# A fused lightning attention and SwiGLU block: dummy matmuls of 512 columns ahead of the first transposes split into four of 128, and three more tiny ones

## The chip, the cores and the metric

The kernel runs on one core of one Trainium2 chip. The metric is the device time of one execution in microseconds; the median of several runs is compared. A profiled execution has a span (from its first to its last instruction) and a time of its own, which is somewhat longer than the span.

## The reference

Attention with a decay per head runs over blocks of 64 positions; a state per head is carried from block to block. Its output goes through a SwiGLU feed-forward block. There are 4 batches, 8 heads, 768 positions and a head dimension of 64; the feed-forward block has 512 inputs, 1536 hidden units and 512 outputs. All inputs and the output are float32.

```
for b in range(12):                      # blocks of 64 positions
    intra = (qb @ kb.T) * Dmask          # Dmask[i,j] = lam**(i-j) for i >= j, else 0
    out_b = intra @ vb + (qb * lam**(pos+1)) @ kv_state
    kv_state = lam**64 * kv_state + (kb * lam**(63-pos)).T @ vb
x = out, as (3072, 512)
g = x @ w_gate
y = (g * sigmoid(g) * (x @ w_val)) @ w_out
```

## The kernel before

The kernel works in blocks of 128 positions and twelve groups, each a pair of blocks of one batch. A group's q and k are loaded in float32 (`load_fp32`, L115), cast to bf16 (`cast_half`, L296, for the first groups), transposed, multiplied into scores (`scores`, L350), masked on VectorE (L357), and multiplied with v (`intra`, L515). The sum over earlier blocks comes from a state per head (`upd_mm` at L408, `inter` at L502). The feed-forward block of earlier groups (gate at L558, value at L574, output at L593, L703 and L793) fills TensorE between the attention of later groups.

Each engine executes its instructions in the order in which the program lists them; the order is written out by hand. The instructions of the start are issued in this order:

- The loads of lam, q, k and v for groups 0 and 1, on the queues of SyncE and ScalarE.
- On TensorE: 30 tiny dummy matmuls (L181) that multiply a constant, 64 rows by 64 columns of weights with 8 moving columns, alternately on the two halves of the array; then `warm_up(2)`; then the matmul that spreads lam over the partitions (L183, the wait for the transfer of lam stands before it); then `warm_up(4)`.
- ScalarE takes the logarithm of lam (L195, L197) and makes the decay tables of q (`qdec`, L203); VectorE makes `dec` (L199) and casts the first half of q of group 0 (L296), and ScalarE casts the half of k.
- `pe_transpose(0, 0, warm=1)`: four transposes on TensorE of q (L312), one dummy matmul of 256 columns (L187), four transposes of k (L312). VectorE moves the q transposes to SBUF with the decay factor (L318), ScalarE moves those of k (L314).
- `scores(0, (0,), 3)`: three dummy matmuls of 256 columns (L187) and sixteen score matmuls (L350).

`warm_up` writes dummy results into a bank of PSUM that nobody reads. Each matmul in the program is two instructions on TensorE, a weight load (in the profile PEld) and the matmul itself (PE).

```
    warm = nc.const_aps.tensor(1.0, [128, 512], BF16)
    def warm_up(n, cols=512):
        b = bank()
        for _ in range(n):
            nc.tensor.matmul(b[:, 0:cols], warm[:, 0:128], warm[:, 0:cols], start=True, stop=True)
```

The functions that the change touches, with the line numbers of the profile:

Of the kernel before, what the change touches and what calls it, by code (L numbers as in the profile page):

```python
# [19 lines left out]
@with_exitstack  # L20
def kernel(
    ctx: ExitStack,
    tc: tile.TileContext,
    q: bass.AP,
    k: bass.AP,
    v: bass.AP,
    lam: bass.AP,
    moe_w_gate: bass.AP,
    moe_w_val: bass.AP,
    moe_w_out: bass.AP,  # L30
    out: bass.AP,
):
    nc = tc.nc
    with tc.manual_schedule():
        _body(ctx, tc, nc, q, k, v, lam, moe_w_gate, moe_w_val, moe_w_out, out)


def _body(ctx, tc, nc, q, k, v, lam, moe_w_gate, moe_w_val, moe_w_out, out):
# [46 lines left out]
    def bank():  # L85
        if fixed:
            primed[fixed[0]] = 0
            last_bank.insert(0, fixed[0])
            return banks[fixed.pop(0)]
        last_bank.insert(0, ring[0] % 8)  # L90
        b = banks[ring[0] % 8]
        primed[ring[0] % 8] = 0
        ring[0] += 1
        return b
# [48 lines left out]
# [4 lines that stand above are left out]
# [29 lines left out]

    lam_ps = bank()
    b = bank()
    for n in range(30):
        r = slice(n % 2 * 64, n % 2 * 64 + 64)  # L180
        nc.tensor.matmul(b[r, 0:8], warm[r, 0:64], warm[r, 0:8], start=True, stop=True, skip_group_check=True)  # L181
    warm_up(2)
    nc.tensor.matmul(lam_ps[:, 0:H], ones[:, 0:128], lam_row, start=True, stop=True)  # L183
    warm_up(4)
    def warm_into(b, n, cols=256):
        for _ in range(n):
            nc.tensor.matmul(b[:, 0:cols], warm[:, 0:128], warm[:, 0:cols], start=True, stop=True)  # L187
# [1069 lines left out]
```

## Time and profile before

| what | value |
|---|---|
| runs | 217.79, 217.82, 219.28 us; median 217.82 |
| profiled execution | 218.1 us, span 216.3 us |
| TensorE matmuls (PE) | busy 209.8 us, 97% of the span, 2813 instructions |
| TensorE weight loads (PEld) | busy 153.3 us, 2816 instructions |
| VectorE (DVE) | busy 149.5 us, 69% |
| ScalarE (ACT) | busy 129.1 us, 60% |
| GpSimd (POOL) | busy 92.3 us, 43% |
| dummies of L146 | 6 matmuls of 512 columns, 607 to 634 ns each |

Times in the profile are counted from the first instruction. A row of the timeline has the start, the length from the first start to the last end of a merged group, the engine, the line, the operation, the tiles (output before the arrow) and the number of instructions. Matmuls overlap: the length of a single one is longer than the distance from its start to that of the next, so how fast TensorE works is read from distances of starts. A clock row gives the clock that TensorE was granted, as far as it is recorded.

### The profile page before, as it was taken

To read this page: it belongs to the slowest core of one execution; us is meant where nothing else is said; L and a number is where in the kernel's file an instruction comes from. 1 tells how busy PE (TensorE), PEld (TensorE's weight loads), DVE (VectorE), ACT (ScalarE), POOL (GpSimd) and SP (SyncE) were. 2 spreads that over 40 slices of the span, in tenths; PEclk is the share of its full clock that TensorE was granted. 3 is DMA by queue.
4 is the path that set the end of the run, shared out by engine and by line. 5 is a ranking of instruction groups with operands and counts; after the bars stand their busy time and mean duration, and the time that the engine had idled before them with its cause. 6 is when DMAs were issued, how large, how long until landed. Compare 5 with 4: busy or idle time off the path is not lost.

```text
span 216.3 us, 6883 instructions
## 1 busy us (share of the span) xinstructions
PE 209.8 (97%) x2813; PEld 153.3 (71%) x2816; DVE 149.5 (69%) x267; ACT 129.1 (60%) x280; POOL 92.3 (43%) x126
## 2 busy tenths in 40 slices
PE   8899999999999999999999999999999999999994
PEld 4666455888887447666754545888888888888883
DVE  1774447576677989775478988886797379961760
ACT  5788577666545254638368478754872766636522
POOL 6684755818498240685962336510740022200200
PEclk9999999999999999999999999999999999999999
DMA  6999999999999878999678899481000500005014
GB/s 189 346 354 345 378 337 321 290 249 232 315 352 151 191 214 190 257 186 238 168 169 236 203 230 215 103 225 68 2 5 3 194 0 3 0 3 194 0 52 146
DMA packets 88320, 39.76 MB, mean 184 GB/s; under 512 B 57698, under 2 KB 83938, under 8 KB 88290
## 3 DMA queue, kind: packets, MB, share of 16 engines
q1 hardware_dynamic: 84978, 38.22, 64.9%
q10 hardware_dynamic: 3312, 1.11, 2.0%
q8 instruction: 22, 0.36, 0.7%
q14 instruction: 8, 0.07, 0.1%
HBM read 28.31 MB, written 6.29 MB: 160 GB/s over the span
## 4 chain that ended last, share of the span: by engine, by line
PE 73%; DVE 7%; DMA 6%; SPq 5%; ACT 3%; issue 2%; POOL 2%; POOLq 1%; DVEq 0%
PE bank L793 20%; PE bank L703 15%; PE bank L558 13%; PE bank L574 13%; DMA woraw<-in_moe_w_out_dram 4%; PE bank L593 4%; SPq L122 2%; DMA qraw<-in_q_dram 2%; SPq L247 2%; DVE ws L666 2%; DVE h L577 1%; PE bank L515 1%; PE bank L146 1%; DVE wt L623 1%; PE bank L502 1%
## 5 line engine op out<-in xcount | busy, mean ns | idle before, releaser
L577 DVE TENSOR_TENSOR h<-sil,bank 128x256 bf16<-128x256 bf16 (+1 forms) x67 | 34.8, 531 | 26.3 <-PE bank L574 18.0
L558 PE MATMUL bank<-xt,wg_sb 128*128 128x256 bf16 (+1 forms) x268 | 52.5, 319 | 0.0
L574 PE MATMUL bank<-xt,wv_sb 128*128 128x256 bf16 (+1 forms) x268 | 52.4, 319 | 0.0
L562 ACT ACTIVATE sil<-bank 128x256 bf16<-128x256 f32 (+1 forms) x67 | 31.7, 479 | 23.7 <-PE bank L558 16.8
L574 PEld LDWEIGHTS <-wv_sb 128*128 128x128 bf16 x268 | 26.0, 98 | 15.8 <-DVE wv_sb L988 0.5
L558 PEld LDWEIGHTS <-wg_sb 128*128 128x128 bf16 x268 | 25.2, 98 | 13.8 <-DVE xt L527 0.2
L258 POOL TENSOR_TENSOR v_s<-v,dec 128x512 bf16<-128x512 f32 (+1 forms) x18 | 24.1, 1356 | 24.0 <-DMA v<-in_v_dram 16.0
L733 POOL TENSOR_TENSOR h<-sil,es 128x512 bf16<-128x512 bf16 x6 | 7.0, 1163 | 50.0 <-ACT sil L730 50.0
L793 PEld LDWEIGHTS <-h 128*128 128x128 bf16 x240 | 23.3, 98 | 3.4 <-issue 0.3
L793 PE MATMUL bank<-wo_sb,h 128*128 128x256 bf16 x180 | 21.6, 273 | 0.1
L793 PEld LDWEIGHTS <-hs 128*128 128x128 bf16 x180 | 17.6, 98 | 2.9
L357 DVE TENSOR_TENSOR ssb<-bank,causal 128x512 bf16<-128x512 f32 x24 | 15.4, 681 | 1.8 <-PE bank L350 1.8
L745 DVE TENSOR_TENSOR bank<-bank,es 128x512 f32<-128x512 f32 x12 | 7.8, 693 | 11.4 <-PE bank L703 10.1
L703 PEld LDWEIGHTS <-ws 128*128 128x128 bf16 x144 | 13.8, 97 | 2.3 <-issue 0.2
L793 PE MATMUL bank<-wt,hs 128*128 128x256 bf16 x120 | 15.0, 272 | 0.0
L730 ACT ACTIVATE sil<-bank 128x512 bf16<-128x512 f32 x18 | 10.7, 596 | 7.0 <-POOL h L733 4.6
L463 POOL TENSOR_TENSOR kvf<-kvs,ups 128x256 f32<-128x256 f32 x8 | 6.5, 813 | 19.1 <-ACT ups L430 19.1
L733 DVE TENSOR_TENSOR h<-sil,bank 128x512 bf16<-128x512 bf16 x18 | 12.2, 682 | 1.4 <-ACT sil L730 1.4
L703 PE MATMUL bank<-xs,ws 128*128 128x256 bf16 x96 | 12.8, 272 | 0.0
L527 ACT CAST xt<-bank 128x512 bf16<-128x512 f32 x19 | 11.6, 658 | 2.0 <-PE bank L515 1.5
L463 POOL TENSOR_TENSOR kvf<-kvf,ups 128x256 f32<-128x256 f32 x16 | 12.2, 763 | 0.9
L703 PE MATMUL bank<-xt,wg_sb 128*128 128x256 bf16 x72 | 10.8, 273 | 0.2 <-ACT ups L430 0.2
(119 smaller groups left out, 361.3 us busy)
## 6 DMA issues: line engine op xcount, KB each, us to landing
out_dram<-osb SPq DMA_DIRECT2D x22, 256.0 KB, 2.1
v<-in_v_dram SPq DMA_DIRECT2D x18, 256.0 KB, 4.5
woraw<-in_moe_w_out_dram SPq DMA_DIRECT2D x6, 512.0 KB, 7.6
qraw<-in_q_dram SPq DMA_DIRECT2D x24, 128.0 KB, 3.2
wraw<-in_moe_w_gate_dram SPq DMA_DIRECT2D x5, 512.0 KB, 7.2
wraw<-in_moe_w_val_dram SPq DMA_DIRECT2D x5, 512.0 KB, 6.9
kraw<-in_k_dram SPq DMA_DIRECT2D x20, 128.0 KB, 3.1
kraw<-in_k_dram SPq DMA_DIRECT2D x4, 512.0 KB, 6.6
```

The lines of the kernel that those rows point to most:

```text
L258: eng.tensor_tensor(out=st[("vs", g)][:, h0:h1], in0=st[("v", g)][:, h0:h1].rearrange("p h (s d) -> p h s d", s=2), in1=vfac(g, h0, h1), o ...
L357: nc.vector.tensor_tensor(out=ssb[:, h2, 2 * c:2 * c + 2].rearrange("p a s n -> p a (s n)"), in0=sp[(c, h2)].rearrange("p (a x) -> p a x", ...
L463: nc.gpsimd.tensor_tensor(out=o, in0=f, in1=u, op=ALU.add)
L527: fns[r](out=xt[:, g % 2, :, r].rearrange("p h (m s) -> p h s m", s=2) if g < NAT0 else xt[:, g % 2, :, :, r * M:r * M + M], in_=op[r].rea ...
L558: nc.tensor.matmul(gp[:, 0:N], wg_sb[:, mc, fs], xt[:, b0 // 2:b1 // 2, mc].rearrange("p g b n -> p g (b n)"), start=(mc == 0), stop=(mc = ...
L562: nc.scalar.activation(sil[:, 0:N], gp[:, 0:N], AF.Silu)
L574: nc.tensor.matmul(vp[:, 0:N], wv_sb[:, mc, fs], xt[:, b0 // 2:b1 // 2, mc].rearrange("p g b n -> p g (b n)"), start=(mc == 0), stop=(mc = ...
L577: nc.vector.tensor_tensor(out=h_sb[:, fc % FH, b0:b1].rearrange("p b n -> p (b n)"), in0=sil[:, 0:N], in1=vp[:, 0:N], op=ALU.mult)
L703: nc.tensor.matmul(o[:, fi * 256:fi * 256 + 256], lhs(i, c, 2 * j + fi), rhs(c), start=(start and fi == 0 and c == 0), stop=(c == KH - 1), ...
L730: nc.scalar.activation(sil[key], src, AF.Silu)
L733: eng.tensor_tensor(out=h_of(half, r), in0=v3(sil[half, r]), in1=v3(src), op=ALU.mult)
L793: nc.tensor.matmul(o, lhs(f), rhs(f), start=(start and f == 0), stop=(f == FH - 1), skip_group_check=True)
```

## The change

Three tiny dummy matmuls are added to the 30, and each of the six dummies of 512 columns becomes four of 128. The number of dummy columns in `warm_up` stays (1,024 ahead of the lam matmul, 2,048 behind it); there are 18 more matmuls and 18 more weight loads of this kind, and three more of each of the tiny kind, 42 instructions in all.

```
     lam_ps = bank()
     b = bank()
-    for n in range(30):
+    for n in range(33):
         r = slice(n % 2 * 64, n % 2 * 64 + 64)
         nc.tensor.matmul(b[r, 0:8], warm[r, 0:64], warm[r, 0:8], start=True, stop=True, skip_group_check=True)
-    warm_up(2)
+    warm_up(8, 128)
     nc.tensor.matmul(lam_ps[:, 0:H], ones[:, 0:128], lam_row, start=True, stop=True)
-    warm_up(4)
+    warm_up(16, 128)
```

## The prediction, made before the change was run

> **What bounds the kernel now.** I read first the busy line of the page, because it says which engine could be bought anything.
>
> ```profile
> span 216.3 us, 6883 instructions
> PE 209.8 (97%) x2813; PEld 153.3 (71%) x2816; DVE 149.5 (69%) x267; ACT 129.1 (60%) x280; POOL 92.3 (43%) x126
> PEclk9999999999999999999999999999999999999999
> ```
>
> PE is busy in 97% of the span, so time can only come from what PE does, or from the 6.5 us in which it is idle. The clock row shows full speed everywhere, but it can't show the start: the durations of equal matmuls have to be read for that. The edit lies in the first 5 us, so next comes the timeline of PE there (start, length, line, operation).
>
> ```profile
> 0.84 0.96 PE L181 MATMUL bank<-const-bfloat16-1.0 64*64 64x8 bf16 x30 [0.84 <-PEq L1241]
> 1.74 1.03 PE L146 MATMUL bank<-const-bfloat16-1.0 128*128 128x512 bf16 x2
> 2.71 0.59 PE L183 MATMUL bank<-lam_row,ones 1*128 1x8 f32 x2
> 3.23 1.89 PE L146 MATMUL bank<-const-bfloat16-1.0 128*128 128x512 bf16 x4
> 4.91 0.63 PE L312 MATMUL bank<-ident,qk 128*128 128x128 bf16 x4
> 5.34 0.42 PE L187 MATMUL bank<-const-bfloat16-1.0 128*128 128x256 bf16 x1
> 5.55 0.63 PE L312 MATMUL bank<-ident,qk 128*128 128x128 bf16 x4
> 5.98 0.58 PE L187 MATMUL bank<-const-bfloat16-1.0 128*128 128x256 bf16 x3
> 6.86 0.42 PE L350 MATMUL bank<-qkt 64*64 64x128 bf16 x16 [0.30 <-ACT qkt L314]
> 7.21 0.62 PE L312 MATMUL bank<-ident,qk 128*128 128x128 bf16 x8
> 7.67 0.50 PE L187 MATMUL bank<-const-bfloat16-1.0 128*128 128x256 bf16 x3
> ```
>
> Two things are to be seen. PE has no gap of its own from 0.84 to 6.5, so whatever is put ahead of L312 moves L312. And PE runs at two speeds: four transposes (L312) take 0.43 us from 4.91 to the next row at 5.34, that is 107 ns each, while eight of them at 7.21 take 0.46 us to 7.67, 57 ns each. The 256-column dummies say the same: one takes 0.21 us from 5.34 to 5.55, three take some 0.33 at 7.67. The switch falls among the three dummies at 5.98. So the six 512-column dummies of L146 run at the slow rate, about 0.42 us each (1.68 us from 3.23 to 4.91 for four).
>
> The third view is the chain of waits that ends last, cut to the first 8 us (start, length, what).
>
> ```profile
> 0.84 0.96 PE bank L181 x30
> 1.81 0.97 PE bank L146 x2
> 2.78 0.52 PE bank L183 x2
> 3.30 1.82 PE bank L146 x4
> 5.12 0.43 PE bank L312 x4
> 5.55 0.21 PE bank L187
> 5.76 0.44 PE bank L312 x4
> 6.22 0.58 ACT qkt L314
> 6.81 0.52 ACT qk L296
> 7.33 0.81 ACT qdec L203 x2
> ```
>
> The chain runs through every dummy of the edit. From 6.22 to 12.8 it is mostly ACT and DVE, and from 12.8 on mostly PE. A delay at L312 is thus passed on one for one at first, and nothing on PE takes it back later.
>
> **The change, part by part.** (1) Three more tiny matmuls at L181, each with its weight load. Thirty pairs take 0.90 us from 0.84 to 1.74, 30 ns a pair, so three cost 0.09 us on the path. Nothing hides them: L146 follows at once.
>
> (2) Two 512-column dummies become eight of 128, and four become sixteen. The columns stay 1,024 and 2,048. What is added are 18 matmuls and 18 weight loads, with the six in (1) the 42 instructions of the title. What a 128-column pair costs at the slow rate is shown by L312 itself, which is just such a pair with a fresh 128x128 load before each: 107 ns. Eight are 0.86 us, against two at 0.42 = 0.84; sixteen are 1.71, against 1.68. That is +0.05 us together. The load of a pair is hidden under the columns of the matmul before it. If that cover were gone, 18 loads at their own length would be added:
>
> ```profile
> L146 PEld LDWEIGHTS <-const-bfloat16-1.0 x6: 103/116/151, 1.7 to 4.1; 128*128 128x128 bf16 x6
> ```
>
> 18 times 116 ns is 2.1 us, the upper end of this edit. Its lower end is a little below nothing: if the pairs ran at the rate of the later transposes, 57 ns, the 24 of them would take 1.37 us instead of the 2.52 us of six 512-column ones, a gain of 1.15; that needs the fast clock, which no row before 5.98 shows, so it is a rival below and not a property of the shape. I take +0.05, because L312 at 4.91 is the same instruction in form, at the same clock, and next to the place.
>
> The Trainium skill, page TensorE: Matmul & The Clock Gate, section LDWEIGHTS (loading the stationary operand), speaks against the split: a load costs the number of weight columns at the slow rate, 107 ns for 128. Added in full 18 times, that would be 1.9 us by the page. The trace shows that the load does not stand in line: L312 repeats load and matmul every 107 ns altogether. The sum goes by the trace.
>
> (3) What the shift makes late. The lam matmul (L183) begins about 0.1 us later (0.09 + 0.02), and with it ACT's ln (L195 at 3.34), the exponent tables (L203) and DVE's dec (L199, 3.62 to 3.89), behind which the first q cast (L296) stands in DVE's order. That cast now runs 3.92 to 4.39; 0.1 later it ends near 4.49, still ahead of the transposes, which start at 4.91 + 0.14 = 5.05. The second half of the transposes needs ACT's k cast, which ended at 5.26 and will end near 5.37, against a start near 5.69. So L312 stays bound by PE's own order, and L314 at 6.22 moves to some 6.36. No DMA is added or moved; no wait is added; no bank is taken differently, since the number of calls stays.
>
> Sum: 0.09 + 0.05 = +0.14 us at L312. The waits behind it (POOL's v_s on a v transfer until 6.99, DVE's second q cast on its transfer at 5.28) may swallow some, so between 0 and 0.14, and I take 0.1. The profiled execution had 218.1 us with a span of 216.3; it becomes 218.2. The three runs have a median of 217.82, 0.3 below the profiled one, and 0.1 on top of that gives **217.9 us**. Between the runs shown lie 1.5 us, so about 1% is what a measurement of this kernel can tell from no change; this is far inside.
>
> **The rivals.** A. *The fast clock comes late.* The columns are the same, but what releases the clock is not visible; it could respond to the mix of loads and matmuls, or to PE's first microseconds having moved. The switch happens 5.2 us after PE's first matmul, and directly behind it PE has its gaps:
>
> ```profile
> 6.15:9.56 3.41, 2.51 (x52) 1.00 1.15 346
> 9.56:12.97 3.41, 3.17 (x117) 1.00 1.15 343
> ```
>
> (Stretch, length, PE busy and number of instructions, granted clock, DMA share, GB/s.) If PE misses the switch at 6.1, a stretch with 0.90 us of gaps follows. In it, 12 transposes at 57 ns, 6 dummies at 0.11 and two groups of L350 at 0.2 are 1.7 us of columns at full speed, so half speed adds at most 1.7; the chain is on ACT and DVE there, so much of it may hide: 0.3 at the least (two L350 groups at 0.2 stand between ACT and DVE), and I take 1.0, giving 218.9. If the second stretch is lost too, it adds between 0.6 and 2.4 (32 + 32 + 16 + 8 small matmuls, 12 transposes and 4 dummies are some 2.4 us of columns, with 0.24 us of gaps), say 1.4: **220.3**, slower by over 1%. The case turns slower from the second lost stretch on. For it: the switch really does come just ahead of sparse work, and the slowest run shown, 219.28, is 1.46 above the median, the size of such a loss. Against it: PE's columns from 3.23 to 6.1 are as dense after the edit as before.
>
> The Trainium skill, same page, Part 1: The HAM clock gate (the "warmup" mystery), says the release goes by a free-running activity window of about 3.4 us and not by a count of matmuls, and that the cold count varies from run to run. By that rule, the split alone would change nothing, and a miss would cost one whole window; the trace has one switch only, so it can't tell. That I keep case A as high as I do rests on the rows and the run at 219.28.
>
> B. *The fast clock comes early.* More loads could count as more activity. If PE were fast from 3.3 on, the sixteen pairs would take 0.9 instead of 1.71, and the transposes would wait for the q cast (4.49) and k cast (5.37) instead. The k transposes would end near 5.37 + 0.1 + 4 x 0.057 + the 0.2 of a last matmul's own length = 5.9, against 6.18 now: 0.3 us gained, 217.5. At most, halving all 3.4 us of slow work from 2.7 to 6.1 gives 1.7 and 216.1, if the casts did not bind. For it: PE was busy already at 2.7 and the clock didn't come, so something was missing. Against it: nothing in the rows says that loads count.
>
> C. *The loads are not hidden.* 217.9 + 2.1 - 0.05 = 219.9, just below 1%. Against it stands L312. For it: the dummies write the same 128 columns of one bank again and again, while the four L312 at 4.91 write four different ranges.
>
> D. *The dummies don't matter*, because the transposes wait for data anyway. Then the time stays at 217.8. Against it: the q cast ends at 4.39, and L312 starts at 4.91. It can't be told from the forecast by time.
>
> **How the numbers follow.** Forecast together with D: 0.45. A: 0.28, half of it with one stretch lost (218.9), half with two (220.3). B: 0.18. C: 0.07, half of it beyond 1%. Something not listed: 0.02. Slower by over 1%: 0.14 from A's second stretch, 0.04 from C, 0.04 from the upper end of A's first stretch and of the rest, 0.22. Faster by over 1% would need more than B's bound; I give it 0.06 for a gain that grows in the chain of ACT and DVE from 6.2 to 12.8. Within 1%: 0.72. The range goes from 217.0, which is B with twice its gain against the forecast, to 220.4, just beyond A with two stretches; what is left out are A's upper ends (0.07), B's bound (0.05) and the rest (0.02 to 0.05), less than 2 in 10.
>
> **What would show it.** In the profile after: L181 x33 ending near 1.83; L146 as 8 and 16, each group with 107 ns from start to start; L312 first at 5.05; the length of an L312 transpose falling from 314 to 219 ns near 6.1, as now; ACT's L314 at 6.35. Case A would show long dummies (over 0.4 us) at L187 behind 6.2; B short L312 at their first row; C a pace of over 200 ns in L146. The prediction is wrong if L312's first start moves by 0.14 and the end moves by over 1 us: then the delay is not passed on one for one, but changes something later that the first 8 us don't show.

## The result and the profile after

The changed kernel takes 219.41 us (median of 22 runs, 218.28 to 220.97), the kernel before 218.13 us in the runs beside it (217.38 to 221.66). The ratio is 1.005 with a 95% interval of 1.0025 to 1.0074: slower by 0.5 to 1.6 us. The ratio is that of the means, without the two runs of the kernel before that lie over 1.5% above its fastest, and gives +1.1 us where the medians differ by 1.28. The profiled execution took 218.6 us.

The page of the changed kernel, to be read beside that of before; its queue table (packets, MB, share of 16 engines) lists the transfers that bring instructions:

```profile
span 216.9 us, 6928 instructions
PE 209.7 (97%) x2837; PEld 154.8 (71%) x2837; DVE 146.8 (68%) x267; ACT 129.5 (60%) x280; POOL 92.4 (43%) x126
...
q8 instruction: 22, 0.36, 0.7%
```

TensorE's start, from its timeline:

```profile
0.84 1.04 PE L181 MATMUL bank<-const-bfloat16-1.0 64*64 64x8 bf16 x33 [0.84 <-PEq L1241]
1.81 1.03 PE L146 MATMUL bank<-const-bfloat16-1.0 128*128 128x128 bf16 x8
...
3.31 1.89 PE L146 MATMUL bank<-const-bfloat16-1.0 128*128 128x128 bf16 x16
4.98 0.61 PE L312 MATMUL bank<-ident,qk 128*128 128x128 bf16 x4
...
5.54 0.39 PE L312 MATMUL bank<-ident,qk 128*128 128x128 bf16 x4
...
6.60 0.42 PE L350 MATMUL bank<-qkt 64*64 64x128 bf16 x16 [0.34 <-ACT qkt L314]
```

The dummies cost almost nothing: the first transposes start at 4.98 and not at 4.91, and the shift of 0.07 is that of the three tiny dummies. Eight and sixteen short dummies take as long as two and four long ones (1.81 to 2.78, before 1.74 to 2.71). In this execution the clock switched earlier (the k transposes at 5.54 are already fast), so the first scores start at 6.60, 0.26 us ahead of before. Yet the end is later. The chain that ended last, cut to the first 8 us, now runs through the issue of the loads (L115, 85.3% of it) and no longer through TensorE; it comes to TensorE only at 32.37 us, by way of a later load of q and its cast on GpSimd. The loss first shows on TensorE between 11 and 16 us. First the kernel before:

```profile
11.84 0.39 PE L312 MATMUL bank<-ident,qk 128*128 128x128 bf16 x4
...
13.38 0.22 PE L408 MATMUL bank<-v_s,qk 64*64 64x64 bf16 x4
13.88 0.41 PE L408 MATMUL bank<-v_s,qk 64*64 64x64 bf16 x28 [0.29 <-issue]
...
15.13 0.61 PE L558 MATMUL bank<-xt,wg_sb 128*128 128x256 bf16 x4
```

The same rows of the changed kernel:

```profile
12.50 0.40 PE L312 MATMUL bank<-ident,qk 128*128 128x128 bf16 x4 [0.69 <-POOL qk L296]
...
14.65 0.38 PE L408 MATMUL bank<-v_s,qk 64*64 64x64 bf16 x24 [0.36 <-POOL v_s L258]
...
15.86 0.39 PE L558 MATMUL bank<-xt,wg_sb 128*128 128x256 bf16 x2
```

The last transposes of group 1 (L312) wait 0.69 us for GpSimd's cast of q, the state update (L408) 0.36 us for its scaling of v, and the feed-forward block (first L558) starts 0.73 us later. The steps add up: TensorE is 0.20 us ahead at the dummy before these transposes (11.53 against 11.73), 0.66 behind at them, and 0.73 behind from the state update on. Before the change the rows shown have one idle time, of 0.29 us, put down to "issue": nothing that the profile shows released it. It is gone after. GpSimd's cast of the second half of q of group 1 waits for its transfer. Before and after, from the timelines of GpSimd:

```profile
10.64 0.61 POOL L296 CAST qk<-qraw 128x512 bf16<-128x512 f32 x1
```

```profile
11.83 0.61 POOL L296 CAST qk<-qraw 128x512 bf16<-128x512 f32 x1 [1.32 <-DMA qraw<-in_q_dram]
```

The load was issued at the same time (6.10 us against 6.11) and its data came about 1.2 us later. Later loads are late too: for the transposes of the next group, GpSimd's cast of q comes at 31.70 us and not at 30.73, TensorE waits 0.24 us for it, and the next feed-forward matmuls (L558) start at 33.38 instead of 32.41, 0.97 us late. What moved on the DMA engines is the first of the 22 instruction transfers: in the trace's DMA records it starts at 11.52 us before the change and at 9.26 after it, 16 KB in one packet of 0.93 us. There are 5,629 TensorE instructions on the page of before, so a transfer brings about 256, and 42 more of them ahead shift every boundary between transfers to an earlier place of the program. That gave the theory: **the position of TensorE's instruction stream decides which loads its transfers fall among.** The rivals: the delay at the start is passed on (rival 1), or the split holds back the fast clock (rival 2).

The trace's record of semaphores shows the link directly. Each of these loads raises its semaphore, the counter on which engines wait for it, sixteen times, taken here as sixteen parts. Of the q load issued at 6.1 us, fifteen parts come by 10.56 us before the change and by 10.58 after it; the last comes at 10.59 before and at 11.78 after. The loads behind it each have one late part as well after the change, by 1.0 to 1.2 us. Before the change, the first load with such a part is one of gate weights (fifteen parts by 12.89, the last at 14.04), for which TensorE does not wait in the rows above. So one part in sixteen is held up, and not all of the traffic.

### The profile page after: what moved, and what is told of

Its sections match the earlier page's. It is cut to its first block, busy times and chain, and to the rows that moved or that the text cites. A ratio compares the mean times of both kernels' runs of the same rounds, so it can differ in the third digit from the quotient of the medians.

```text
span 216.9 us, 6928 instructions
## 1 busy us (share of the span) xinstructions
PE 209.7 (97%) x2837; PEld 154.8 (71%) x2837; DVE 146.8 (68%) x267; ACT 129.5 (60%) x280; POOL 92.4 (43%) x126
## 4 chain that ended last, share of the span: by engine, by line
PE 80%; DMA 8%; SPq 6%; ACT 1%; POOL 1%; issue 1%; DVE 1%; POOLq 1%; DVEq 0%
PE bank L793 21%; PE bank L558 16%; PE bank L574 16%; PE bank L703 15%; PE bank L593 5%; DMA qraw<-in_q_dram 4%; DMA wraw<-in_moe_w_val_dram 4%; SPq L115 3%; SPq L233 3%; PE bank L515 2%; PE bank L502 2%; PE bank L408 1%; PE bank L350 1%; ACT sil L730 1%; PE bank L376 1%
## 5 line engine op out<-in xcount | busy, mean ns | idle before, releaser
L558 PE MATMUL bank<-xt,wg_sb 128*128 128x256 bf16 (+1 forms) x268 | 52.5, 319 | 0.0
L558 PEld LDWEIGHTS <-wg_sb 128*128 128x128 bf16 x268 | 25.1, 98 | 13.9 <-ACT wg_sb L241 0.2
L258 POOL TENSOR_TENSOR v_s<-v,dec 128x512 bf16<-128x512 f32 (+1 forms) x18 | 23.0, 1292 | 20.4 <-DMA v<-in_v_dram 11.7
L463 POOL TENSOR_TENSOR kvf<-kvs,ups 128x256 f32<-128x256 f32 x8 | 5.8, 726 | 24.2 <-ACT ups L430 22.2
L463 POOL TENSOR_TENSOR kvf<-kvf,ups 128x256 f32<-128x256 f32 x16 | 12.9, 806 | 0.9
```

Of the source, the lines that this page charges most:

```text
L258: eng.tensor_tensor(out=st[("vs", g)][:, h0:h1], in0=st[("v", g)][:, h0:h1].rearrange("p h (s d) -> p h s d", s=2), in1=vfac(g, h0, h1), o ...
L463: nc.gpsimd.tensor_tensor(out=o, in0=f, in1=u, op=ALU.add)
L558: nc.tensor.matmul(gp[:, 0:N], wg_sb[:, mc, fs], xt[:, b0 // 2:b1 // 2, mc].rearrange("p g b n -> p g (b n)"), start=(mc == 0), stop=(mc = ...
```

## The experiments

Each kernel was timed in five rounds against the kernel before, except the repeat of 42 fewer, which has one run (223.98 us). The table collects one profile of each: TensorE instructions ahead of the first score groups against before, start of the first instruction transfer, of GpSimd's cast of q's second half and of its first v scaling of group 1, start of the feed-forward block (us), and the ratio with its interval.

```
kernel                    instr  transfer  q cast  v scale  ffn    ratio
before                       0    11.52    10.64   11.40   15.13
after                      +42     9.26    11.83   12.54   15.86  1.0050 (1.0025-1.0074)
split only                 +36     9.93    10.66   12.56   15.88  1.0032 (1.0000-1.0063)
tiny only                   +6    11.61    10.64   11.40   15.18  1.0001 (0.9969-1.0033)
count in idle gaps         +42    10.28    10.89   12.90   16.22  1.0031 (0.9996-1.0066)
split, count kept            0    11.79    10.62   11.39   15.34  1.0001 (0.9966-1.0036)
count at the end             0    11.56    10.69   11.51   15.12  1.0017 (0.9989-1.0045)
one dummy less              -2    11.57    10.59   11.35   15.24  1.0002 (0.9969-1.0035)
ten tiny fewer             -20    11.70    10.63   11.39   15.19  1.0035 (1.0004-1.0065)
22 tiny for one long       -42    12.38    10.57   11.32   16.32  1.0101 (1.0058-1.0144)
after, 42 more in gaps     +84     9.42    11.96   12.70   16.02  1.0065 (1.0034-1.0097)
```

**The two halves of the change.**

```
 # split only
-    for n in range(33):
+    for n in range(30):      # the rest as changed
 # tiny only: range(33), warm_up(2) and warm_up(4) as before
```

> The split alone, 30 tiny dummies as before: 36 more TensorE instructions ahead of the first transposes. Theory (position of TensorE's instruction stream: the first 16 KB transfer of instructions starts about 2 us earlier, at 9.3 us and not at 11.5, and delays the second half of q for group 1): as the changed kernel, 0.8 to 1.3 us slower than before, GpSimd's cast of that half near 11.8 us and not at 10.65. Rival 1 (the start is late by some hundredths of a us and that is passed on): 0 to +0.1 us, the cast at 10.7. Rival 2 (the split makes the fast clock come later): +1 us, but with the cast at 10.7 or moved by no more than the clock's switch.

> Three more tiny dummies alone, the dummies of 512 columns as before: 6 more TensorE instructions. Theory (position of the instruction stream): the first transfer of instructions moves by some tenths of a us only, to about 11 us, so the q half lands nearly as before: 0 to +0.3 us. Rival 1 (delay at the start): +0.1 us. Rival 2 (the split and the clock): 0.

The split alone starts its feed-forward block 0.75 us later, though its first transposes start at 4.91 as before (its time agrees, 1.0032, but the interval begins at 1.0000); the tiny ones alone, which do move them to 4.99, move the feed-forward block by 0.05 us. Rival 1 can't account for the loss. In the split kernel the transfer came at 9.93, and the cast of q was on time, against the expectation; it is v that came late (fifteen parts by 11.39, the last at 12.49), and TensorE waits for its scaling:

```profile
14.66 0.38 PE L408 MATMUL bank<-v_s,qk 64*64 64x64 bf16 x24 [0.75 <-POOL v_s L258]
```

**The count without the split, and the split without the count.**

```
 # count in idle gaps: before, and ahead of the scores of group 0
+    scores(0, (0,), 3, 8)     # 8 tiny dummies on one quarter of the array
+    scores(0, (1,), 3, 13)    # 13
 # split, count kept: after, with
+    for n in range(11):       # tiny, not 33
+    warm_up(1)                # one dummy of 512 columns
+    ring[0] -= 1              # the next dummies use its bank again
     warm_up(8, 128)
```

> The kernel before with 21 tiny dummies (42 TensorE instructions) put where TensorE waits anyway: 8 ahead of the first scores (idle near 6.5 us) and 13 ahead of the second (idle near 8.2 us). The first transposes keep their place and the dummies of 512 columns are whole. Theory (position of the instruction stream): as the changed kernel, 0.8 to 1.3 us slower, transfer of instructions near 9.3 us and the cast of q's second half near 11.8. Rivals 1 and 2 (delay at the start; the split and the clock): 0 to +0.1 us.

> The changed kernel with the split kept, but 11 tiny dummies and one of 512 columns in the place of 33 tiny ones, so that as many TensorE instructions stand ahead of the first transposes as before the change. Theory (position of the instruction stream): the transfer of instructions near 11.4 us, the cast of q's second half at 10.6, and a time within 0.3 us of before. Rival 2 (the split and the clock): 1.1 us slower than before, as the changed kernel. Rival 1 (delay at the start): the first transposes start 0.2 us earlier, so 0.2 faster than the changed kernel's forecast, within 0.2 of before.

With whole dummies and the first transposes untouched at 4.91, 42 instructions in idle gaps delay GpSimd's scaling of v by 1.5 us and the feed-forward block by 1.09. The transfer came at 10.28 us and not near 9.3, so here too v was hit and not, as expected, q. Its time agrees (1.0031), but the interval touches 1. With the split kept and the count restored, the loads are on time and the ratio is 1.0001, although full speed came at 7.7 us in its profile, 1.5 us later than before; rival 2 falls. There the idle time put down to issue is back, in the same place as before (this kernel's L410 is L408 before):

```profile
14.10 0.41 PE L410 MATMUL bank<-v_s,qk 64*64 64x64 bf16 x28 [0.37 <-issue]
```

**The count where no early boundary moves.** 21 tiny dummies behind the last matmul:

> The kernel before with 42 more TensorE instructions behind its last real matmul, where only the last stores run. Theory (what counts is where the 16 KB transfers of instructions fall among the first loads): no earlier boundary moves, so the transfer stays near 11.5 us, GpSimd's v scaling of group 1 starts at 11.4 us, and the time is that of before within 0.2 us. Rival (42 instructions more cost about 1 us wherever they stand, for instance through the length of the program): 0.8 to 1.1 us slower.

The first 16 us are those of before, and the ratio, 1.0017, holds 1 in its interval. The number of instructions alone does not cost 1 us.

**Fewer instructions, and more.** 22 tiny dummies replaced by one of 512 columns (-42); ten tiny ones dropped (-20); the changed kernel with 42 more in the gaps (+84).

> The kernel before with 22 tiny dummies replaced by one of 512 columns, 42 TensorE instructions fewer, and nearly the same length of dummy work. Theory (a threshold: the transfer costs only where it falls ahead of the last load of group 1): transfer near 12 us, no wait for the v scaling, and a time within 0.3 us of before. Rival (the cost is proportional to the number of instructions): 0.8 to 1.1 us faster than before.

> The changed kernel with 42 more tiny instructions in TensorE's idle gaps ahead of the first two score groups, 84 more than before the change. Theory (a threshold): the first transfer of instructions starts near 8 us, one packet of 0.9 us is still all that the loads of group 1 wait for, so as the changed kernel: 0.8 to 1.3 us slower than before. Rival (proportional to the number): 1.8 to 2.2 us slower.

Twice the count costs about as much as once (the intervals overlap), with the same two delays. The transfer came at 9.42 us, not near 8 as expected: TensorE has its own waits on the way, so a position in the stream is not a time. The cost goes with where the transfer falls, not with the count. But the expectation for 42 fewer failed: it is the slowest of all. The loads are on time, and TensorE stands without a wait:

```profile
14.66 0.25 PE L408 MATMUL bank<-v_s,qk 64*64 64x64 bf16 x7 [0.91 <-issue]
```

This is the other side of the same thing: **TensorE has run out of instructions.** Counting the rows of PE and PEld from 0, this idle time stands ahead of row 445 in every kernel that has it: before (0.29), tiny only (0.26), count kept (0.37), count at the end (0.28), and here (0.91). It ends 2.3 to 2.4 us after the start of the first transfer. In all 14 profiles that transfer starts 1.7 to 2.9 us after TensorE starts row 189, 256 rows ahead: that is how instructions put in ahead bring it forward. In 42 fewer, a second one of 2.18 us stands ahead of row 1469, four times 256 further. The row stays and the program moves: 42 instructions are 21 pairs, and the idle time moved from behind the 4th to behind the 25th of the 32 pairs of L408. Two further runs tested that:

> The kernel before with 20 tiny dummies in the place of 30, 20 TensorE instructions fewer. If TensorE runs out of instructions at a fixed place of its stream (instruction 445 of the trace, 14 pairs into the 32 of L408) until 2.3 us after the first transfer of instructions starts: idle time without a cause of 0.4 to 0.8 us there, more than the 0.29 of before and less than the 0.91 with 42 fewer, and 0.1 to 0.6 us slower than before. If fewer instructions ahead of the first transposes only bring the start forward: 0 to 0.3 us faster.

> A second look at the kernel with 42 TensorE instructions fewer. If the place in the stream decides: again idle time without a cause of 0.7 to 1.0 us at L408 after 25 of its 32 matmuls, and the feed-forward block starting after 15.4 us. If the first look was chance: no such idle time over 0.3 us.

With 20 fewer, TensorE stops behind the 14th pair, as expected, but for 0.26 us only, not 0.4 to 0.8: on the way it also waits for GpSimd's scaling of v, and goes on from that at 13.51. Its feed-forward block starts as before (15.19); its ratio of 1.0035 comes from later and is not explained. The repeat of 42 fewer had the same two stops (0.85 at L408, 2.69 at L515) and the feed-forward block at 15.74. In the first profile each stop was followed by a stretch at half clock (stretch, length, busy time of the engines, granted clock, DMA share, GB/s):

```profile
14.95:18.36 3.41, 3.41 (x49) 2.05 (x49) 0.73 (x1) 1.31 (x4) 1.84 (x3) 0.50 1.10 387
...
55.90:59.30 3.40, 3.40 (x17) 2.33 (x17) 1.15 (x2) 0.77 (x2) 2.67 (x5) 0.50 1.07 398
```

In the repeat only the stop near 55 us had such a stretch, so the 16.32 in the table holds some half clock. A stop of a microsecond or two can thus cost up to 1.7 us more (half of 3.41) through the clock. It need not: the five runs of 42 fewer over which the ratio is taken had a granted clock of 0.998 or 1.000, so no such stretch.

**A better start.** One of four long dummies behind the lam matmul dropped (`warm_up(3)`):

> The kernel before with three instead of four dummies of 512 columns behind the lam matmul. The first transposes, which start at 4.91 us although their q was cast at 4.39, start at 4.5; those of k wait for their cast (5.26). Instructions: two fewer, so the transfer stays near 11.5 us. If the chain of the first 6 us is passed on: 0.3 us faster than before. If group 1's loads set the pace from 10.6 us on, whatever the start does: within 0.1 us of before.

```profile
4.48 0.63 PE L312 MATMUL bank<-ident,qk 128*128 128x128 bf16 x4
```

The first transposes start 0.43 us earlier and the feed-forward block does not (15.24 against 15.13; ratio 1.0002). This run does not show that the loads take the gain: full speed came only at 8.3 us in its profile, and the second scores already start at 8.87, 0.16 us later than before. It also has a stop of 0.79 us ahead of row 1469. Other profiles show where a better start is lost: after the change TensorE is 0.20 us ahead at 11.53 and then waits for the loads; with 42 fewer it is 0.27 ahead at L408 (13.11) and then stops for instructions.

**The loads taken away.** The kernel before and the changed one without the loads of group 1's k; group 1 uses the k of group 0, so its own scores are left out:

```
-            load_fp32(g, nc.sync, k, "kraw", ...)
+            if g: st[("kraw", 1)] = st[("kraw", 0)]
+            else: load_fp32(g, nc.sync, k, "kraw", ...)
```

> The kernel before without the loads of group 1's k (512 KB fewer among the first loads); group 1 uses group 0's k in its place, so that part of the result is left out. Theory (the loads of group 1 set the pace until 13 us): q's second half and v of group 1 land about 1.5 us earlier, but TensorE still runs out of instructions near the same place (no-cause idle of 0.3 us or more ahead of instruction 445), so it gains little: 0 to 0.8 us faster than before. Every theory expects this kernel only as the base of the next one.

> The changed kernel with the same load left out. Theory (the transfer of instructions at 9.3 us costs only through the loads of group 1 that it delays): with loads 1.5 us ahead the waits of TensorE for GpSimd's cast (0.69) and scaling (0.36) are gone, and so is the no-cause idle; the feed-forward block starts at the same time or up to 0.5 us earlier than in the kernel before without that load. Rival (the 42 instructions cost in another way): it starts 0.7 us later, and the time is about 1 us more than that kernel's, as between the changed kernel and the one before.

TensorE in the first (L411 is L408 before, L561 is L558), and then in the second:

```profile
13.90 0.41 PE L411 MATMUL bank<-v_s,qk 64*64 64x64 bf16 x28 [0.50 <-issue]
...
15.14 0.61 PE L561 MATMUL bank<-xt,wg_sb 128*128 128x256 bf16 x4
```

```profile
13.44 0.45 PE L411 MATMUL bank<-v_s,qk 64*64 64x64 bf16 x32
...
15.09 0.61 PE L561 MATMUL bank<-xt,wg_sb 128*128 128x256 bf16 x4
```

With slack in the loads, the early transfer (10.10 us) delays nobody here: v of group 1 is there at 10.79, and the first load with a late part is again one of gate weights. The stop for instructions is gone, and the 0.73 us between the two feed-forward blocks is gone too (-0.05). The times, 0.9961 (0.9924 to 0.9997) and 0.9980 (0.9934 to 1.0025) of the kernel before, do not separate the two: the second profile loses 1.4 us against the first between 90 and 100 us. No kernel tried beats both of the original ones with the whole computation.

## Why the prediction was right or wrong

The range held the time (219.41 within 217.0 to 220.4) and within 1% was the likeliest outcome. The size was not right: +0.1 us was forecast, and the ratio says +1.1 (0.5 to 1.6).

- **Price of the dummies.** Parts (1) and (2) were right in kind and a little high: 0.14 was summed, 0.07 measured. Sixteen pairs of 128 columns take 1.67 us (3.31 to 4.98), 104 ns each, so the loads are hidden and rival C did not occur. The Trainium skill, page TensorE: Matmul & The Clock Gate, section LDWEIGHTS (loading the stationary operand), gives the length of a load, by its rule 107 ns here (102 to 152 in the trace); the estimate of 1.9 us came from adding it in full, and that the trace rules out.
- **The step that failed** is in part (3): "No DMA is added or moved". An instruction transfer was moved, by 2.3 us. It lay in the queue table all along, as a row that names no line of the program, and I read issues by line only. The term missing from the sum is +0.73 us at the feed-forward block: 0.86 lost from the dummy at 11.53 to the transposes behind it (0.69 of it the idle time for the cast), 0.07 more at the state update (a wait of 0.36 in the place of a stop of 0.29), less the 0.20 by which TensorE was ahead.
- **"Nothing on PE takes it back later"** was wrong too. A shift at the start is passed on for a while (0.20 us ahead at 11.53 after the change), but then the waits for the loads or for instructions swallow it. Rival D, that the transposes wait for data anyway, did not occur: they moved with the dummies, to 4.98 here and to 4.48 with one dummy less.
- **Rivals A and B, the clock.** Over the profiles the switch came between 4.7 us (42 fewer) and 8.3 us (one dummy less), and in the repeat of 42 fewer it came at 6.9 (6.1 before, 5.4 after the change). The same program thus gave an early and a late switch; the edit did not decide it. The Trainium skill, page TensorE: Matmul & The Clock Gate, Part 1: The HAM clock gate (the "warmup" mystery), has a free-running window of about 3.4 us and a cold start that varies from run to run. The traces agree: the half-clock stretches above last 3.41 us and start 40.96 us apart (14.95 and 55.91 in the clock's record), twelve times as much, and the two runs of one program switched 2.2 us apart. That the slowest early run, 219.28, was a late switch was a guess that nothing here bears out.
- **The test that I named** for being wrong, that the first transposes move by 0.14 and the end by over 1 us, is about what happened (0.07, and +1.1 by the ratio).

The Trainium skill, page Runtime: NRT & Kernel Launch, section Instruction fetch mechanics, says that instructions come in 16 KiB blocks of 256, fetched by the sequencer's own DMA queue, and that the cost of a boundary is mostly hidden. The traces agree with the first half (22 transfers, a step of 256). The second half holds for most blocks, but not for all: two of the 22 were not hidden with 42 fewer, and the stops over all profiles were 0.26 to 2.69 us. A load made late by 1.2 us is a cost of another kind.

**What stays open.** In 13 of the 14 profiles (with 84 more, parts are late earlier too) no load has a part more than 0.3 us late until the first instruction transfer starts, and the first load with a late part (by 1.0 to 1.5 us) was due 0.6 to 1.5 us after that start. That the shared thing is a DMA engine is argued from this one part in sixteen; the records don't name the engine, and 1.2 us behind a packet of 0.93 is not fully accounted for. How 0.73 us at the feed-forward block becomes +1.1 in the ratio is not shown either: in the profiled executions the distance is 0.97 at 33 us and 0.57 at the end. Past 90 us TensorE has idle times of 0.5 to 1.6 us in changing places (0.64 at 134 us with the count at the end, for GpSimd's scaling of v; 1.57 at 135 with 84 more, for a DMA transpose; 0.86 and 0.93 at 124 and 127 with ten tiny fewer, for VectorE), in kernels with and without an early shift; what decides these was not found, and they are why the times separate less well than the first 16 us do.

## What to carry to other kernels

Instructions are a load like any other: TensorE's come in blocks of 256 through the same DMA engines, so adding or dropping instructions, dummies above all, moves every later block, and what matters is what each block then collides with. Too early, and it lands among the loads that set the pace; too late, and TensorE stands still in a stretch of small matmuls, and the clock may fall behind it. When an edit changes a count, list the instruction transfers, and look for idle time of TensorE that nothing releases.

## What was not expected of the hardware

- TensorE stops for want of instructions at a fixed place of its stream, rows 445 and 1469 of its trace (1,024 apart), and goes on 2.3 to 2.4 us after the transfer starts at the first, 3.2 to 3.3 us at the second in both profiles of 42 fewer. The packet took 0.93 to 0.96 us at the first and 1.8 at the second there, so TensorE goes on 1.3 to 1.5 us after its end each time.
- Behind the first instruction packet, one part in sixteen of a load comes late by 1.0 to 1.5 us, and the next loads keep most of that delay (1.19 to 1.00 us over five loads after the change).
- Stops of 0.91 and 2.18 us each had a stretch of 3.41 us at clock 0.50 behind them in one profile; one of 0.85 us in another had none.
- The time at which TensorE first reaches full speed varied between 4.7 and 8.3 us over the profiles, without a visible tie to the dummies.
